# A buffer for each slot's row lists, the next slot's gathers ahead of the output writes, and a single tile's first product in two PSUM tiles

## The chip, the core and the metric

The kernel runs on one NeuronCore of a Trainium2 chip. Its engines work side by side, each through its own instructions in order: TensorE (PE in the profile; its weight loads are shown as PEld), VectorE (DVE), ScalarE (ACT), GpSimd (POOL) and SyncE (SP), which here issues most of the DMA transfers. GpSimd issues the indirect ones, which gather or scatter rows by a list of row numbers. Semaphores tie the engines together. The metric is the device time of one execution in microseconds (us).

## The reference

Attention with four sink tokens and a window of 128, over 4 batches, 8 heads, 768 positions and 64 dimensions, feeds a mixture of experts that gives each of the 3072 tokens to one of 8 experts:

```python
keep = is_sink | in_window                      # sink: pos < 4; window: 0 <= rel < 128
scores = np.where(keep, scale * q @ k.T, -1e9)
a = np.exp(scores - max); a = a / (a.sum(-1) + 1e-9)
x = (a @ v) -> (3072, 512)
...
logits = x @ w_gate                             # (3072, 8)
e_idx = argmax(logits); gate_w = softmax(logits)[e_idx]
eom = 1 / (1 + exp(-(x @ w_output_gate)))
for e in range(8):
    mask = e_idx == e
    h = np.maximum(x[mask] @ w1[e], 0)          # 512 -> 1024
    out[mask] = gate_w[mask, None] * eom[mask, e, None] * (h @ w2[e])   # 1024 -> 512
```

## The kernel before

**Stages.** The first half of the span is attention, a pair of heads at a time (`pair_step`), which leaves the token rows in a DRAM buffer `xd`, each with its output factor as a last column. Routing runs beside it. From about 180 us on experts are worked on, at first between the last attention steps, and from about 280 us on alone. Within the block around the whole stage (`manual_schedule`, L1285) each engine's instructions are issued in the order in which the program states them, so a line that stands earlier in the Python code stands earlier in its engine's queue.

**Work units.** `plan` (L720) lists the units of expert work. Entries 0 to 3 are early ones: 256 rows of each of the four experts that have most tokens. Entries 4 to 16 are thirteen slots of fixed size, which the device fills with experts at run time. `SIZES` (L37) counts a slot in units of 64 rows: 6 (three tiles of 128 rows), 4 (two tiles), 2 (one tile, a "single") and 1 (half a tile, a "half"). `SEQ` (L38) sets their order; by plan entry the tiles are 4: 3, 5: half, 6: 3, 7: single, 8: 2, 9: half, 10: 2, 11: single, 12: 2, 13: half, 14: 2, 15: single, 16: half. The last runs only where it is needed (L1434).

**Steps.** `steps` (L725 to L731) has for each entry a `first` (the product with w1 and the relu) and a `second` (the product with w2 and the writes). Products are made of three float32r products each, of high and low parts. `slots` (L1231) walks the steps. Between the pieces of a step it also places, at set times, the transposes of the next entry's rows (`to_x`, whose pieces are x_parts, L526, or half_x, L679). At the end of a step in which such transposes were placed it calls `rows_of` (L1193) for the entry after that one.

**Row lists.** `rows_of(k)` first lets SP load the row lists of entries up to k + 2 (`load_ids`, L736, L744 to L748: from the DRAM table `unitd` into the tile `idx`), those that are not there yet; then it issues the gathers of entry k (`gather`, L514): one indirect DMA of 128 rows per tile, on GpSimd, into one of three `xg` buffers (`XB`). Column 0 of a list serves the gather, column 1 or 2 the write. All slots' lists are parts of one tile, `idx` (L330).

**Writes.** `mm2_parts` (L662) yields behind each of 8 parts of the second product, and then, when it is asked once more, calls `put` (L652) for each tile: ScalarE scales the result into one of four `y` buffers, and GpSimd scatters it to `out` with an indirect DMA (L655). A three-tile entry makes its third tile's product and write first, the other two behind it.

**GpSimd's other work.** Weights come from DRAM by SP into four staging buffers (`raw`, L493). ScalarE casts the high part (L503), and VectorE, or GpSimd for one chunk in four, subtracts for the low part (L504). A split frees the staging buffer for the next load. The splits are placed between the steps' pieces by `supply` (L1041), by modelled times written into the program.

**The single tile.** `single_parts` (L611) makes the w1 product of one tile with the rows as the stationary side: two products of 512 columns, `products(0, ...)` and `products(1, ...)` (L616 to L622), each followed by a relu on VectorE (L602) and by a transpose (`turn`). Both write into one PSUM tile of two banks, which `s_tile` (L546) takes from a ring of two.

Of the kernel before, what the change touches and what calls it, by code (L numbers as in the profile page):

```python
# [10 lines left out]
I32 = mybir.dt.int32  # L11
# [7 lines left out]
P = 128  # L19
# [17 lines left out]
SIZES = (6, 6, 4, 4, 4, 4, 2, 2, 2, 1, 1, 1, 1)  # L37
SEQ = (0, 9, 1, 6, 2, 10, 3, 7, 4, 11, 5, 8, 12)  # L38
NSLOT = len(SIZES)
NT_MAX = 3  # L40
# [14 lines left out]
def moe_kernel(tc, qT, kx, vx, vs, wgo, w1, w2, nsink, window, out):  # L55
# [5 lines left out]
    nc = tc.nc  # L61
    ctx = ExitStack()
    with ctx:
        const = ctx.enter_context(tc.tile_pool(name="const", bufs=1))
        rt = ctx.enter_context(tc.tile_pool(name="rt", bufs=1))
# [261 lines left out]

        idx_e = rt.tile([P, 2, NE, 2], I32, name="idx_e")

        idx = rt.tile([P, NSLOT, NT_MAX, 4], I32, name="idx")  # L330
        lin_i = rt.tile([P, NSLOT], I32, name="lin_i")
        io8n = const.tile([P, E], F32, name="io8n")
        nc.vector.tensor_scalar(out=io8n, in0=io8, scalar1=float(NJP), scalar2=None, op0=ALU.mult)
# [180 lines left out]
        def gather(mp, ids, n=NTOK):  # L514
            xg = mp.tile([P, XW], F32, name="xg", bufs=XB)
            nc.gpsimd.indirect_dma_start(out=xg, out_offset=None, in_=xd[0:n + 1, :],  # L516
                                         in_offset=bass.IndirectOffsetOnAxis(ap=ids[0], axis=0))
            return xg, mp.tile([P, 1], F32, name="sc", bufs=6)
# [27 lines left out]
        def s_tile():  # L546
            return ps_s.tile([P, 2, 512], F32, name="s")

        def hidden(mp, xs):
            return [mp.tile([P, 2, xs[0].shape[-1]], F32R, name=name, bufs=4) for name in ("hh", "hl")]  # L550
# [49 lines left out]
        def relu(mp, ps):  # L600
            hr = mp.tile([P, 4, P], F32, name="hr", bufs=2)
            nc.vector.tensor_scalar(out=hr, in0=ps.rearrange("p (a b) -> p a b", b=P), scalar1=0.0, scalar2=None, op0=ALU.max)  # L602
            return hr

        def turned(hr):
            tp = ps_t.tile([P, 4, P], F32, name="tp")
            for f in range(4):
                nc.tensor.transpose(out=tp[:, f, :], in_=hr[:, f, :], identity=ident)
            return tp

        def single_parts(mp, w, xs, hs):  # L611

            (wh, wl), (xh, xl) = w, xs
            both = s_tile()

            def products(q, ds):  # L616
                qs = slice(q * 512, (q + 1) * 512)
                for d in ds:
                    wd, wld = wh[d][:, qs], wl[d][:, qs]
                    for i, (x, a) in enumerate(((xh, wd), (xh, wld), (xl, wd))):  # L620
                        nc.tensor.matmul(out=both[:, q, :], lhsT=x[:, d, 0:P], rhs=a,
                                         start=d == 0 and i == 0, stop=d == ND - 1 and i == 2)  # L622

            def turn(hr):
                tp = turned(hr)
                for a in range(2):
                    hi, lo = (x[:, :, 0:P] for x in hidden(mp, xs))
                    tpa = tp[:, 2 * a:2 * a + 2, :]
                    nc.scalar.copy(out=hi, in_=tpa)
                    tt(out=lo, in0=tpa, in1=hi.bitcast(F32), op=ALU.subtract)  # L630
                    hs.extend((hi[:, f, :], lo[:, f, :]) for f in range(2))

            products(0, range(2))
            yield
            products(0, range(2, ND))
            h0 = relu(mp, both[:, 0, :])
            yield
            products(1, range(3))
            yield
            turn(h0)  # L640
            products(1, range(3, ND))
            h1 = relu(mp, both[:, 1, :])
            yield
            turn(h1)

# [73 lines left out]

        plan = [(order_i[0:1, r:r + 1], [(idx_e[:, 0, r, j:j + 1], idx_e[:, 1, r, j:j + 1]) for j in range(2)], False) for r in range(NE)]  # L720
        for q in SEQ:
            cols = [[idx[:, q, i, j:j + 1] for j in range(3)] for i in range(-(-SIZES[q] // 2))]
            plan.append((exp_i[0:1, q:q + 1], cols, SIZES[q] == 1, q))
        n = len(plan) - 1
        steps = []  # L725
# [7 lines left out]
        queue = [k for f, k in steps if f == "first" and k > 2] + [n]  # L733
        there = set()

        def load_ids(q):  # L736

            at = nc.sync.value_load(lin_i[0:1, q:q + 1], min_val=0, max_val=(E - 1) * NJP + NJ)
            z = SIZES[q]
            for a in range(2):  # L740
                r = slice(a * U, (a + 1) * U)
                if z == 1:
                    src = unitd[:, bass.ds(at, 1), :]
                    nc.sync.dma_start(out=idx[r, q, 0:1, 0:2], in_=src[:, :, 0:2])  # L744
                    nc.sync.dma_start(out=idx[r, q, 0:1, 2:3], in_=src[:, :, 2 + a:3 + a])
                else:
                    src = unitd[:, bass.ds(at, z), :].rearrange("u (i a) c -> u i a c", a=2)
                    nc.sync.dma_start(out=idx[r, q, 0:z // 2, 0:2], in_=src[:, :, a, 0:2])  # L748


        mctx = ctx.enter_context(ExitStack())
# [10 lines left out]
        with ExitStack() as actx:  # L762
# [173 lines left out]
            def point(name=None):  # L936

                if later and name in (None, later[0][1]):
                    x = later[0]
                    x[1] = next(x[0], None)  # L940
                    if x[1] is None:
                        later.remove(x)
# [116 lines left out]
            def ensure(key):  # L1059
                while not all(x["key"] != key for x in items[n_put[0]:]) or key in todo:  # L1060
                    if n_put[0] == len(items):
                        while later:
                            point()
                        assert build()
                    place()
# [20 lines left out]
            def early_gather(k):  # L1086
                done = [after for after, m in ROUNDS for _ in range(m)][k] + 1
                return [gather(mx, [idx_e[:, 0, k, j:j + 1]], done * S) for j in range(2)]
# [104 lines left out]
            def rows_of(k):  # L1193
                ids = plan[k][1]
                while later and k >= NE:
                    point()
                for j in range(max(k, NE), min(k + AHEAD, len(plan))):
                    if j not in there and not later:
                        there.add(j)
                        load_ids(plan[j][3])  # L1200
                xgs[k] = early_gather(k) if k < NE else [gather(mx, a) for a in ids]
# [29 lines left out]
            def slots():  # L1231


                rest = None
                for i, (f, k) in enumerate(steps):
                    ensure((k, 0 if f == "first" else 1))
                    parts, costs = first(k) if f == "first" else second(k)
                    whole = sum(c for c, _ in costs)
                    tasks = []
                    if rest is not None:  # L1240
                        tasks.append((1.2, rest))
                        rest = None
                    j = queue[0]
                    follows = steps[i + 1:i + 3]
                    x = None
                    if plan[j][2]:
                        if j < len(plan) - 1 and f == "first" and follows[0] == ("first", j):
                            x = to_x(j)
                    elif f == "second" and ("first", j) in follows and not plan[k][2]:
                        x = to_x(j)  # L1250
                    if x is not None:
                        m = len(xgs[j])
                        end = whole - (0 if follows[0] != ("first", j) else 2.4)
                        tasks += [(max(0.1, end - 1.5 * (m - a)), x) for a in range(m)]
                    tasks.sort(key=lambda z: z[0])
                    t = 0.0
                    for n, (c, done) in enumerate(costs):
                        next(parts)
                        t += c
                        for _ in range(2):  # L1260
                            if tasks and tasks[0][0] <= t:
                                next(tasks.pop(0)[1], None)
                        yield c, done
                    for z in tasks:
                        next(z[1], None)
                    if f == "first" and len(xgs[k]) == 1:
                        rest = parts
                    else:
                        assert next(parts, None) is None
                    if x is not None:  # L1270
                        assert next(x, None) is None
                        queue.pop(0)
                        rows_of(queue[0])
                while n_put[0] < len(items) or todo:
                    if n_put[0] == len(items):
                        assert build()
                    place()
# [7 lines left out]
            with tc.manual_schedule(engines={ET.PE, ET.Activation, ET.DVE, ET.Pool, ET.SP}):  # L1285
                for i in range(NP + 2):
                    if i == NP:
                        qctx.close()
                        mp = mctx.enter_context(tc.tile_pool(name="mp", bufs=2, side="right", reuse_waits="tile"))
# [196 lines left out]
```

## Time and profile before

| | us |
|---|---|
| median of 3 runs | 582.18 (578.35 to 582.23) |
| the profiled execution | 580.31 |
| its span in the profile | 578.5 |
| TensorE busy | 513.3 (89%) |
| VectorE, ScalarE, GpSimd busy | 330.5, 269.5, 257.9 |
| TensorE's last product | 567.1 to 567.5 |

How to read the rows in the prediction. A row of the timeline has the start in us from the beginning of the span, the duration, the engine, the line of the kernel, the operation, output<-inputs and how often it follows in a row; in brackets the idle time of the engine just before it and what ended it. A row of the waits has the engine, the operation that waited, what it waited for, and then the sum in us, the number of waits and the longest. Releasers are inferred: where one instruction waits for several things, the row names the one that came last by the profile, which can be the wrong one. A row of the windows has the stretch in us and its length, then each engine's busy time with the number of instructions (PE, PEld, DVE, ACT, POOL), the granted TensorE clock as a share of full speed, the mean busy share of the 16 DMA engines, and what they moved in GB/s.

### The profile page before, as it was taken

How to read it: one execution, taken by the hardware profiler on the slowest of the kernel's cores; microseconds unless marked ns; L12 is line 12 of the kernel's file. 1: busy time of each engine (PE TensorE's matmuls, PEld its weight loads, DVE VectorE, ACT ScalarE, POOL GpSimd, SP SyncE). 2: the span in 40 equal slices, each digit the busy share in tenths (PEclk: the TensorE clock that was granted, in tenths of full speed). 3: DMA queues.
4: the chain of work that ended last, by engine and by line, in shares of the span. 5: the costliest groups of instructions: out<-in, count | busy, mean ns of one | idle time of the engine just before them, and what ended most of it. 6: DMA issues, size and time to landing. Idle time of an engine off the chain costs nothing. (4 is left out here: it accounts for less than half of the span.)

```text
span 578.5 us, 10477 instructions
## 1 busy us (share of the span) xinstructions
PE 513.3 (89%) x3432; PEld 390.0 (67%) x3432; DVE 330.5 (57%) x752; ACT 269.5 (47%) x721; POOL 257.9 (45%) x312
## 2 busy tenths in 40 slices
PE   3999999999979998998999999995999984799992
PEld 1566656666656753848899688984867964777971
DVE  5567698698867768994633424441644642544520
ACT  2576666666647220444534335541545442345420
POOL 4557756857856322635353313342512531513420
PEclk9999999999989998999999999998999996999997
DMA  6166775568987886337778665476586684866760
GB/s 228 61 134 187 145 151 169 142 139 213 192 247 121 205 210 205 106 113 256 229 226 312 240 195 156 139 264 246 183 291 214 226 267 178 265 224 224 253 227 19
DMA packets 72496, 112.83 MB, mean 195 GB/s; under 512 B 12044, under 2 KB 38672, under 8 KB 72434
## 3 DMA queue, kind: packets, MB, share of 16 engines
q1 hardware_dynamic: 67970, 98.16, 58.6%
q0 software_dynamic: 4464, 13.91, 6.6%
q8 instruction: 30, 0.49, 0.4%
q14 instruction: 32, 0.26, 0.2%
HBM read 98.28 MB, written 13.45 MB: 193 GB/s over the span
## 5 line engine op out<-in xcount | busy, mean ns | idle before, releaser
L833 ACT ACTIVATE e<-s,nmx 128x132 f32<-128x132 f32 x192 | 69.5, 366 | 67.2 <-DVE nmx L831 56.6
L821 PE MATMUL s<-kr,qr 64*128 64x260 f32 (+1 forms) x384 | 63.1, 430 | 16.2 <-ACT e L833 10.8
L821 PEld LDWEIGHTS s<-kr,qr 64*128 64x128 f32 x384 | 30.5, 198 | 40.2 <-ACT e L833 28.4
L544 DVE SCALAR_TENSOR_TENSOR hl<-s,hh 128x512 fp32r<-128x512 f32 (+1 forms) x32 | 24.2, 757 | 58.2 <-ACT hh L543 52.8
L655 POOL DMA_INDIRECT out_dram<-y,idx x20 | 24.4, 1219 | 59.1 <-DMA idx<-unitd 14.5
L543 ACT ACTIVATE hh<-s 128x512 fp32r<-128x512 f32 (+1 forms) x32 | 20.9, 652 | 61.7 <-PE s L563 56.5
L831 DVE TENSOR_REDUCE nmx<-s 128x2 f32<-128x264 f32 x96 | 41.5, 432 | 3.3
L537 DVE TENSOR_TENSOR xl<-tp,xh 128x512 fp32r<-128x512 f32 x21 | 14.4, 689 | 45.0 <-ACT xh L536 45.0
L808 POOL TENSOR_SCALAR qr<-qr 128x256 f32<-128x256 f32 x48 | 39.9, 850 | 0.4 <-DMA qr<-in_qT_dram 0.4
L85 POOL TENSOR_SCALAR_AFFINE_SELECT g<-f 128x512 f32<-128x512 f32 (+1 forms) x48 | 28.3, 589 | 21.7 <-DVE f L850 19.0
L833 ACT ACTIVATION_READ_ACCUMULATOR e<-s,nmx 128x1 f32 x192 | 37.6, 196 | 0.0
L827 DVE COPY_PREDICATED s<-maskf,s 128x256 f32<-128x256 int32 x80 | 33.7, 421 | 6.8 <-PE s L821 6.8
L844 PE MATMUL tp<-ident,e 128*128 128x128 f32 x192 | 30.2, 297 | 0.4 <-ACT f L848 0.4
L844 PEld LDWEIGHTS tp<-ident,e 128*128 128x128 f32 x192 | 22.1, 149 | 11.9 <-issue 4.7
L536 ACT CAST xh<-tp 128x512 fp32r<-128x512 f32 x21 | 12.3, 587 | 35.8 <-PE tp L534 35.8
L85 POOL TENSOR_SCALAR_AFFINE_SELECT f<-f 128x512 f32<-128x512 f32 (+1 forms) x48 | 27.0, 563 | 3.3
L655 POOL DMA_INDIRECT out_dram<-y,idx_e x8 | 10.0, 1254 | 39.0 <-ACT y L654 22.3
L534 PE MATMUL tp<-ident,xg 128*128 128x128 f32 x84 | 13.8, 291 | 14.9 <-DMA xg<-xd,idx 14.9
L516 POOL DMA_INDIRECT xg<-xd,idx x21 | 22.1, 1051 | 10.8 <-issue 5.5
L891 PE MATMUL oA<-f,vt 128*64 128x128 f32 x256 | 26.5, 285 | 0.4
L534 PEld LDWEIGHTS tp<-ident,xg 128*128 128x128 f32 x84 | 11.2, 151 | 19.0 <-issue 16.7
L848 ACT COPY f<-tp 128x512 f32<-128x512 f32 x32 | 18.6, 582 | 0.4 <-PE tp L844 0.4
(652 smaller groups left out, 1558.2 us busy)
## 6 DMA issues: line engine op xcount, KB each, us to landing
raw<-in_w_dram SPq DMA_DIRECT2D x88, 512.0 KB
kr<-in_kx_dram SPq DMA_DIRECT2D x16, 396.0 KB
qr<-in_qT_dram SPq DMA_DIRECT2D x16, 384.0 KB
vt<-in_vx_dram SPq DMA_DIRECT2D x16, 384.0 KB
xd<-x SPq DMA_DIRECT2D x16, 384.0 KB
a0h<-in_w_dram SPq DMA_DIRECT2D x4, 512.0 KB
a0l<-in_w_dram SPq DMA_DIRECT2D x4, 512.0 KB
b0h<-in_w_dram SPq DMA_DIRECT2D x3, 512.0 KB
```

Source lines behind the costliest of these rows:

```text
L85: nc.gpsimd.affine_select(out=ap, in_=ap if src is None else src, pattern=pattern, compare_op=op, fill=fill, base=base, channel_multiplier=cm)
L516: nc.gpsimd.indirect_dma_start(out=xg, out_offset=None, in_=xd[0:n + 1, :], in_offset=bass.IndirectOffsetOnAxis(ap=ids[0], axis=0))
L534: nc.tensor.transpose(out=tp[:, d, :], in_=xg[:, d * P:(d + 1) * P], identity=ident)
L544: nc.vector.scalar_tensor_tensor(out=lo, in0=ps, scalar=0.0, in1=hi.bitcast(F32), op0=ALU.max, op1=ALU.subtract)
L655: nc.gpsimd.indirect_dma_start(out=where, out_offset=bass.IndirectOffsetOnAxis(ap=ids, axis=0), in_=y, in_offset=None, bounds_check=rows - ...
L808: nc.gpsimd.tensor_scalar(out=q, in0=q, scalar1=SCALE, scalar2=None, op0=ALU.mult)
L821: nc.tensor.matmul(out=s[:, a, o0:P + CW], lhsT=z["q"][r, t * P:(t + 1) * P], rhs=z["k"][r, k0:k0 + P + CW - o0], start=True, stop=True)
L827: nc.vector.copy_predicated(out=both[:, :, 4:CW], mask=bc(maski[:, 1, 4:CW], 1, 2), data=s[:, :, 0:P])
L831: nc.vector.tensor_reduce(out=m, in_=both, axis=AX.X, op=ALU.max, negate=True)
L833: nc.scalar.activation(out=z["e"][:, t, a, :], in_=both[:, a, :], func=AF.Exp, bias=m[:, a:a + 1], scale=1.0, accum_out=z["rs"][:, t, a:a ...
L844: nc.tensor.transpose(out=tp[:, k, :], in_=z["e"][:, 2 * j + k // 2, k % 2, 4:CW], identity=ident)
L891: nc.tensor.matmul(out=o, lhsT=v[:, kt, r], rhs=src[:, kt, a, :], start=t == kt == 0 or t == kt + 1 == 4, stop=False, skip_group_check=True)
```

## The change

Three edits. First, `idx` becomes a list of tiles, one for each slot; the loads, gathers and writes index it accordingly. Second, at the end of a step in `slots`, the end of the transposes and `rows_of` for the next entry now stand ahead of the last piece of the step's own product, which for a `second` step holds the writes. Third, `single_parts` takes two tiles from the PSUM ring, and uses one bank of each, where it took one tile and used both its banks.

```diff
-        idx = rt.tile([P, NSLOT, NT_MAX, 4], I32, name="idx")
+        idx = [rt.tile([P, NT_MAX, 4], I32, name="idx%d" % q) for q in range(NSLOT)]
...
         def single_parts(mp, w, xs, hs):
 
             (wh, wl), (xh, xl) = w, xs
-            both = s_tile()
+            both = [s_tile()[:, 0, :] for _ in range(2)]
 
             def products(q, ds):
...
-                        nc.tensor.matmul(out=both[:, q, :], lhsT=x[:, d, 0:P], rhs=a,
+                        nc.tensor.matmul(out=both[q], lhsT=x[:, d, 0:P], rhs=a,
                                          start=d == 0 and i == 0, stop=d == ND - 1 and i == 2)
...
-            h0 = relu(mp, both[:, 0, :])
+            h0 = relu(mp, both[0])
...
-            h1 = relu(mp, both[:, 1, :])
+            h1 = relu(mp, both[1])
...
         for q in SEQ:
-            cols = [[idx[:, q, i, j:j + 1] for j in range(3)] for i in range(-(-SIZES[q] // 2))]
+            cols = [[idx[q][:, i, j:j + 1] for j in range(3)] for i in range(-(-SIZES[q] // 2))]
...
-                    nc.sync.dma_start(out=idx[r, q, 0:1, 0:2], in_=src[:, :, 0:2])
-                    nc.sync.dma_start(out=idx[r, q, 0:1, 2:3], in_=src[:, :, 2 + a:3 + a])
+                    nc.sync.dma_start(out=idx[q][r, 0:1, 0:2], in_=src[:, :, 0:2])
+                    nc.sync.dma_start(out=idx[q][r, 0:1, 2:3], in_=src[:, :, 2 + a:3 + a])
...
-                    nc.sync.dma_start(out=idx[r, q, 0:z // 2, 0:2], in_=src[:, :, a, 0:2])
+                    nc.sync.dma_start(out=idx[q][r, 0:z // 2, 0:2], in_=src[:, :, a, 0:2])
...
                     for z in tasks:
                         next(z[1], None)
+                    if x is not None:
+                        assert next(x, None) is None
+                        queue.pop(0)
+                        rows_of(queue[0])
                     if f == "first" and len(xgs[k]) == 1:
                         rest = parts
                     else:
                         assert next(parts, None) is None
-                    if x is not None:
-                        assert next(x, None) is None
-                        queue.pop(0)
-                        rows_of(queue[0])
```

## The prediction

> **What bounds the kernel now.** I read the page first, for the engine that fills the span.
>
> ```profile
> PE 513.3 (89%) x3432; PEld 390.0 (67%) x3432; DVE 330.5 (57%) x752; ACT 269.5 (47%) x721; POOL 257.9 (45%) x312
> ```
>
> TensorE is busy 89% of the span; no other engine passes 57%. So an edit counts by the TensorE idle time it removes, or makes, in the stretch it touches. All edited code belongs to the expert slots, which run from about 280 us on. So the second view is TensorE's waits in that stretch: total us, number, longest.
>
> ```profile
> PE tp L534 <- DMA xg<-xd,idx: 14.9, 2, 8.9
> PE tp L684 <- DMA xg<-xd,idx: 5.6, 3, 3.6
> PE s L621 <- DVE hr L602: 3.0, 3, 1.5
> ```
>
> Five waits for gathered token rows (xg) make 20.5 us; three inside the single-tile product make 3.0 us. Nothing in this list waits for weights. The third view is TensorE in order of time, cut to the rows with a large wait (start, duration, operation, idle before it and its releaser):
>
> ```profile
> 401.79 1.09 PE L534 MATMUL tp<-ident,xg 128*128 128x128 f32 x4 [5.99 <-DMA xg<-xd,idx]
> ...
> 471.61 0.50 PE L621 MATMUL s<-a0h,xh 128*128 128x512 f32 x1 [1.46 <-DVE hr L602]
> ...
> 484.71 1.08 PE L534 MATMUL tp<-ident,xg 128*128 128x128 f32 x4 [8.87 <-DMA xg<-xd,idx]
> ...
> 505.07 0.46 PE L684 MATMUL tp<-ident,xg 64*128 64x64 f32 x4 [3.57 <-DMA xg<-xd,idx]
> ```
>
> The rows wanted at 401.79 are plan entry 8's, at 484.71 entry 12's (each behind a single-tile slot, which is short), at 505.07 entry 13's. The fourth view is GpSimd in order of time, to see why these gathers were late.
>
> ```profile
> 384.62 2.39 POOL L504 TENSOR_TENSOR c4l<-raw,c4h 128x1024 fp32r<-128x1024 f32 x1 [5.31 <-ACT sc L531]
> 388.34 1.00 POOL L655 DMA_INDIRECT out_dram<-y,idx  x1 [1.33 <-ACT y L654]
> 393.54 0.98 POOL L655 DMA_INDIRECT out_dram<-y,idx  x1 [4.20 <-DMA idx<-unitd]
> 394.83 0.99 POOL L516 DMA_INDIRECT xg<-xd,idx  x1 [0.30 <-issue]
> ...
> 467.46 2.42 POOL L504 TENSOR_TENSOR b0l<-raw,b0h 128x1024 fp32r<-128x1024 f32 x1 [5.89 <-ACT b0h L503]
> 470.44 1.39 POOL L655 DMA_INDIRECT out_dram<-y,idx  x1 [0.56 <-ACT y L654]
> 476.69 0.98 POOL L655 DMA_INDIRECT out_dram<-y,idx  x1 [4.86 <-DMA out_dram<-y,idx]
> 477.98 0.99 POOL L516 DMA_INDIRECT xg<-xd,idx  x1 [0.30 <-issue]
> ```
>
> GpSimd works in program order. Two output writes stand ahead of each gather, and the second starts only 5.2 us (393.54 - 388.34) or 6.25 us (476.69 - 470.44) after the first: it waits for the first one's data to land, since both write `out`. The row at 393.54 names a load of row lists (idx) instead, but in the program that load comes behind the write, which cannot wait for it; I read it as the wait of the other row. The gather, ready long before, goes out 0.30 us behind the second write. That is the whole delay.
>
> **The moved gathers.** Ten of the `second` steps now ask for the next rows ahead of their last writes: 14 gathers, of entries 4, 5, 7, 8, 9, 11, 12, 13, 15 and 16. Only five waits exist to be removed; I take them in turn. From issue to landing a gather takes (min, median, max):
>
> ```profile
> DMA to landing us min/median/max: 3.9/5.8/7.5
> ```
>
> *Entry 8.* The gather follows c4l, which ends at 384.62 + 2.39 = 387.01, by 0.30: issued at 387.3 instead of 394.83. It lands between 391.2 and 394.8. TensorE wants it at 401.79 - 5.99 = 395.8, or, if the single-tile wait of the same slot goes too (one of the two under 1.46; about 0.8), at 395.0. Gain 6.0, nothing left.
>
> *Entry 12.* It follows b0l, which ends at 469.88: issued at 470.2 instead of 477.98. TensorE wants it at 475.84, or at 474.4 without the 1.46. It lands between 474.1 and 477.7, so between 0 and 3.3 us are left. What the DMA engines do in these stretches decides where between (columns behind the engines: granted clock, DMA share, GB/s):
>
> ```profile
> 386.00:388.00 2.00, 2.00 (x10) 1.64 (x10) 1.74 (x2) 1.47 (x2) 1.01 (x1) 1.00 0.21 80
> ...
> 396.00:398.00 2.00, 0.00 (x0) 0.00 (x0) 0.70 (x2) 0.00 (x0) 0.97 (x1) 1.00 0.97 348
> ...
> 470.00:472.00 2.00, 0.55 (x3) 0.34 (x3) 1.56 (x2) 0.74 (x2) 1.39 (x1) 1.00 0.35 136
> ...
> 480.00:482.00 2.00, 0.00 (x0) 0.00 (x0) 0.00 (x0) 0.00 (x0) 0.24 (x1) 0.50 1.01 381
> ```
>
> The late gathers met full DMA engines (0.97 and 1.01); the new places are ahead of those weight loads, at 0.21 and 0.35. I take a landing nearer to the shortest, about 5 us: 1.0 us is left, gain 7.9.
>
> *Entries 13, 9 and 5.* Each gather takes the place of a write in front of it:
>
> ```profile
> 310.88 1.03 POOL L655 DMA_INDIRECT out_dram<-y,idx_e  x1 [0.15 <-issue]
> ...
> 317.42 0.99 POOL L516 DMA_INDIRECT xg<-xd,idx  x1 [0.30 <-issue]
> ...
> 412.65 1.82 POOL L655 DMA_INDIRECT out_dram<-y,idx  x1 [0.15 <-issue]
> 414.78 0.97 POOL L516 DMA_INDIRECT xg<-xd,idx  x1 [0.30 <-DVE hl L544]
> ...
> 495.56 1.82 POOL L655 DMA_INDIRECT out_dram<-y,idx  x1 [0.17 <-issue]
> 497.69 1.83 POOL L516 DMA_INDIRECT xg<-xd,idx  x1 [0.30 <-issue]
> ```
>
> Entry 13 moves up 2.1 us against a wait of 3.57. If it lands as slowly as now 1.4 are left, at the median of 5.8 nothing; I take 0.7, gain 2.9. The other two waits at L684 are 5.6 - 3.57 = 2.0 together; entry 5 moves up 6.5 and entry 9 by 2.1, more than their waits. Gain 2.0.
>
> *The clock.* Behind the three long waits the granted clock is half:
>
> ```profile
> 401.70:406.50 4.80, 4.71 (x16) 3.94 (x17) 1.30 (x3) 1.72 (x5) 0.00 (x0) 0.50 0.00 1
> ...
> 484.60:489.20 4.60, 4.49 (x19) 3.84 (x19) 1.12 (x2) 1.52 (x5) 0.00 (x0) 0.57 0.00 0
> ...
> 505.00:510.00 5.00, 4.92 (x28) 4.74 (x28) 0.00 (x0) 0.56 (x2) 0.00 (x0) 0.66 1.04 395
> ```
>
> Busy time times the missing clock: 4.71 x 0.50 + 4.49 x 0.43 + 4.92 x 0.34 = 6.0 us. It appears behind waits of 3.57 us and more and not around the 1.46 (1.00 in the row from 470), so with at most about 1 us left it goes: 6.0. [...]
>
> *What the move costs.* The writes start about 1.3 us later per gather (0.99 + 0.30) where their y was ready. No one on the path reads `out`; what stands behind the writes on GpSimd is the weight splits (L504), and a split frees a staging buffer for which SP's next weight load waits. The tightest place:
>
> ```profile
> 449.75 0.99 POOL L516 DMA_INDIRECT xg<-xd,idx  x1 [0.30 <-issue]
> 453.04 1.00 POOL L655 DMA_INDIRECT out_dram<-y,idx  x1 [2.30 <-DMA out_dram<-y,idx]
> 454.06 2.43 POOL L504 TENSOR_TENSOR a2l<-raw,a2h 128x1024 fp32r<-128x1024 f32 x1
> ...
> SPq L493 <- POOL a2l L504: 4.8, 1, 4.8
> ...
> ACT c3h L503 <- DMA raw<-in_w_dram: 1.7, 1, 1.7
> ```
>
> Today the gather at 449.75, entry 11's, hides in a wait between two writes; ahead of both it pushes a2l, the load that waits 4.8 for it, and perhaps the cast that waits 1.7 for data, by up to 1.3 us. Entries 7's and 15's gathers lie between the same two kinds of write, so the bound is three times this, 3.9, and 0 from below: a write gains nothing from going later. I take 0.5, nearer to 0, because TensorE's list above has no wait for a cast or a split, even behind that 1.7. The other instructions of `rows_of` (register loads and row-list loads, all on SP) keep their place on SP, where the writes issue nothing.
>
> One thing speaks against entry 12's new place. Indirect DMAs take GpSimd 0.97 or 1.83 us in the rows above, and VectorE is busy with a split just there:
>
> ```profile
> 469.61 1.35 DVE L504 TENSOR_TENSOR b1l<-raw,b1h 128x1024 fp32r<-128x1024 f32 x1 [2.13 <-ACT b1h L503]
> ```
>
> The gather may be held to its end at 470.96, up to 0.8 us; the 0 to 3.3 left over covers it. [...]
>
> **A buffer per slot.** It adds no instruction. What it can remove is a wait of one slot's list load on another slot's reads, or the reverse.
>
> ```profile
> 389.30 1.49 SPq L748 DMA_DIRECT2D idx<-unitd  x2
> ```
>
> This load goes out at 389.3, though the write at 393.54, ahead of it in the program, has yet to read another slot's columns of the same buffer. So slots already pass one another, and every gather above shows only the 0.30 of its issue. Cost and gain 0. If the reversed order made the writes wait on the loads, separate buffers would prevent just that.
>
> **Two buffers in the single tile.** The second half's first product waits today until VectorE has read the first half, though it writes other columns: the row at 471.61. With two tiles that read is no longer in its way; VectorE's 0.7 us then lies beside nine products until the turn wants it. The second tile is the other buffer of a ring of two, whose last reader (a hidden-layer relu, or a write's scaling) finished a whole phase earlier. Gain 3.0.
>
> **Sum.** 6.0 + 7.9 + 2.9 + 2.0 + 6.0 + 3.0 - 0.5 = 27.3 us. What follows the last product (567.5 to 578.5) stays. The profiled execution took 580.31 us, 1.8 beyond its span and 1.9 below the median of the runs. It becomes 553.0; the median becomes 582.18 - 27.3 = 554.9. I forecast 555.
>
> **Rivals.** *Stalls shrink but stay.* If the earlier gathers meet weight loads and take 7.5, entry 12 keeps 3.3 and its slow clock (1.9), entry 13 keeps 1.4, and with TensorE running ahead the weight loads, which used the stalls at full DMA share, come due. Against the last: in 401.7 to 406.5 and 484.6 to 489.2 DMA stood at 0.00, all that was asked for having landed. If half of the 27 goes, 568.5.
>
> *It does not do what it says.* The moved gathers wait for something that shows only at the earlier time, such as row lists on SP behind weight loads, or a buffer. Lists are asked for two entries ahead, which speaks against it. Then the single-tile 3.0 remains: 579.
>
> *Slower: gathers block the writes.* A gather waits for one of three xg buffers, and now the writes, the splits and the weight loads stand behind it. One gather of today shows such a wait:
>
> ```profile
> 326.43 0.95 POOL L516 DMA_INDIRECT xg<-xd,idx  x1 [4.74 <-DMA raw<-in_w_dram]
> ...
> 325.21 0.46 PE L684 MATMUL tp<-ident,xg 64*128 64x64 f32 x4 [1.14 <-DMA xg<-xd,idx]
> ```
>
> (It names a weight load; the transposes that free its buffer ran just before, at 325.21.)
>
> Some 4.7 us at each of ten places and on to TensorE would cost 47, less 27: 602. It decides from 2.7 us a place on. Against it: the reading transposes are issued ahead of each moved gather, and only three-tile entries (4, among the moved) need all buffers.
>
> **From cases to numbers.** The sum as it stands 0.72, shrunken stalls 0.16, without effect 0.05, slower 0.07. The sum's own range: with nothing left over and no cost (27.3 + 1.0 + 0.7 + 0.5 = 29.5) and from the fastest run of before, 578.35, it is 548.9; with 3.3 left and its 1.9 of clock, 1.4 left and 3.9 cost, 19.0 remain (27.3 - 2.3 - 1.9 - 0.7 - 3.4): 563.2. To hold 8 in 10 the range goes into the shrunken case: 549 to 570. A change under 1%, 5.8 us, I call no change. Faster 0.88, same 0.05, slower 0.07.
>
> **What would show it.** Right: L534 and L684 wait under 3 us together for xg, the L621 waits are gone, each moved gather's row stands ahead of its writes, the clock shows no half-speed stretch after 390 us, except past the last product. Wrong: waits of TensorE for casts (L503) or splits (L504); a gather with some us of idle ahead of it and the writes behind; a DMA share near 1 with L534 still waiting.

## The result

The changed kernel takes 556.36 us (median of 4 runs, 555.80 to 556.95) against 580.26 us of the kernel before (4 runs, 576.67 to 582.23): 0.9595 of its time, 95% interval 0.9537 to 0.9653. Two later rounds of the same kernel gave 0.9562 [0.9507, 0.9617] and 0.9677 [0.963, 0.9725]. By the three pairs of medians it saves 23.9, 23.2 and 19.2 us. The ratios are taken from fast executions alone (a few fall into a slower state) and the medians from all, so a ratio is not quite the quotient of two medians. The profiled execution took 555.8 us, with a span of 554.1 (578.5 before).

Of the profile after, first the page's line of busy times:

```profile
PE 508.3 (92%) x3432; PEld 386.6 (70%) x3432; DVE 334.1 (60%) x752; ACT 269.3 (49%) x721; POOL 260.2 (47%) x312
```

TensorE does the same 3432 products in a span 24.4 us shorter; its busy time is 5.0 us less, mostly since fewer of them run at half clock (6.0 us of it before by the prediction's count, 1.7 now). TensorE's waits from 270 us on (total us, number, longest), whole up to a last one of 0.3:

```profile
PE tp L684 <- DMA xg<-xd,idx: 2.6, 2, 1.6
PE oA L710 <- ACT y L654: 1.6, 2, 0.8
PE tp L534 <- DMA xg<-xd,idx: 1.1, 1, 1.1
```

Of 20.5 us of waits for gathered rows 3.7 are left, and the three waits of L621 are gone. TensorE in order of time, the three rows that still wait for a gather (entries 9, 12 and 13):

```profile
409.87 0.46 PE L684 MATMUL tp<-ident,xg 64*128 64x64 f32 x4 [1.04 <-DMA xg<-xd,idx]
...
465.32 0.63 PE L534 MATMUL tp<-ident,xg 128*128 128x128 f32 x4 [1.08 <-DMA xg<-xd,idx]
...
481.81 0.46 PE L684 MATMUL tp<-ident,xg 64*128 64x64 f32 x4 [1.57 <-DMA xg<-xd,idx]
```

Entry 8 does not wait at all. GpSimd in order of time, at the two places that the prediction showed:

```profile
383.38 2.39 POOL L504 TENSOR_TENSOR c4l<-raw,c4h 128x1024 fp32r<-128x1024 f32 x1 [4.67 <-ACT sc L531]
385.93 0.99 POOL L516 DMA_INDIRECT xg<-xd,idx  x1 [0.16 <-issue]
387.23 0.97 POOL L516 DMA_INDIRECT xg<-xd,idx  x1 [0.30 <-issue]
388.50 1.02 POOL L655 DMA_INDIRECT out_dram<-y,idx  x1 [0.30 <-issue]
395.38 1.00 POOL L655 DMA_INDIRECT out_dram<-y,idx  x1 [5.86 <-ACT xh L536]
...
457.38 2.40 POOL L504 TENSOR_TENSOR b0l<-raw,b0h 128x1024 fp32r<-128x1024 f32 x1 [5.70 <-ACT b0h L503]
459.93 1.80 POOL L516 DMA_INDIRECT xg<-xd,idx  x1 [0.15 <-issue]
462.04 0.97 POOL L516 DMA_INDIRECT xg<-xd,idx  x1 [0.30 <-issue]
463.31 1.02 POOL L655 DMA_INDIRECT out_dram<-y,idx  x1 [0.30 <-ACT hh L629]
469.08 1.00 POOL L655 DMA_INDIRECT out_dram<-y,idx  x1 [4.74 <-PE oA L673]
```

The gathers stand directly behind the splits c4l and b0l, ahead of both writes. The writes are still 6.9 and 5.8 us apart (388.50 to 395.38, 463.31 to 469.08), each pair under other releasers' names than before. The profile has landing times for the first of each pair, 6.0 and 5.0 us behind its issue, and the second starts 0.8 us behind that: it waits for the first to land, as it did, but the gather that stood behind it in each pair is gone from there. One stretch of half clock is left, and the windows show it (stretch and its length, busy time and instructions of PE, PEld, DVE, ACT and POOL, granted clock, DMA share, GB/s):

```profile
480.00:482.00 2.00, 0.43 (x6) 0.23 (x5) 0.69 (x1) 0.79 (x2) 0.97 (x1) 1.00 0.96 326
...
484.00:486.00 2.00, 2.00 (x12) 2.00 (x11) 0.00 (x0) 0.00 (x0) 0.00 (x0) 0.50 1.01 345
```

It is behind entry 13's wait of 1.57 us, where the DMA share is 0.96 and 1.01.

To see where the time went, the same instructions of TensorE in both profiles (a transpose is a product with the identity, lines L534 and L608):

| TensorE reaches | before, us | after, us | difference |
|---|---|---|---|
| a transpose early in the expert stretch | 302.40 | 303.07 | +0.7 |
| a transpose ahead of entry 8's wait | 384.68 | 383.91 | -0.8 |
| the second transposes of entry 8 | 406.09 | 396.17 | -9.9 |
| a transpose between entry 9's and 12's waits | 435.94 | 425.81 | -10.1 |
| a transpose behind entry 12's wait | 488.82 | 467.75 | -21.1 |
| a transpose behind entry 13's wait | 515.11 | 491.85 | -23.3 |
| the end of the last product | 567.48 | 543.12 | -24.4 |

Nearly all of it comes at two places, entries 8 (9.1) and 12 (11.0), and some at entry 13 (2.2).

### The profile page after: what moved, and what is told of

Its sections match the earlier page's. It is cut to its first block, busy times and chain, and to the rows that moved or that the text cites. A ratio compares the mean times of both kernels' runs of the same rounds, so it can differ in the third digit from the quotient of the medians.

```text
span 554.1 us, 10479 instructions
## 1 busy us (share of the span) xinstructions
PE 508.3 (92%) x3432; PEld 386.6 (70%) x3432; DVE 334.1 (60%) x752; ACT 269.3 (49%) x721; POOL 260.2 (47%) x312
## 4 chain that ended last, share of the span: by engine, by line
PE 46%; DVE 17%; DMA 16%; ACT 8%; issue 7%; POOL 4%; SPq 1%; POOLq 0%; ACTq 0%; DVEq 0%
PE s L563 15%; PE oA L673 5%; DMA out_dram<-y,idx 5%; PE oB L673 5%; ACT e L833 4%; PE s L821 3%; DMA xg<-xd,idx 3%; DMA raw<-in_w_dram 3%; PE s L588 3%; DVE s L827 2%; DMA psk<-hl 2%; DVE nmx L831 2%; PE oA L710 2%; PE s L694 2%; PE oA L891 2%
## 5 line engine op out<-in xcount | busy, mean ns | idle before, releaser
L544 DVE SCALAR_TENSOR_TENSOR hl<-s,hh 128x512 fp32r<-128x512 f32 (+1 forms) x32 | 24.2, 756 | 54.3 <-ACT hh L543 52.1
L655 POOL DMA_INDIRECT out_dram<-y,idx x20 | 23.1, 1155 | 60.3 <-ACT hh L543 11.2
L516 POOL DMA_INDIRECT xg<-xd,idx x21 | 26.3, 1250 | 10.3 <-ACT xf L685 4.7
L655 POOL DMA_INDIRECT out_dram<-y,idx_e x8 | 9.1, 1136 | 34.9 <-ACT y L654 16.7
L654 ACT ACTIVATE y<-oA,sc 128x512 f32<-128x512 f32 (+1 forms) x16 | 10.4, 649 | 17.5 <-issue 4.6
L891 PEld LDWEIGHTS oA<-f,vt 128*64 128x64 f32 x256 | 14.4, 136 | 6.1 <-issue 3.3
```

What stands on the lines that cost most here:

```text
L655: nc.gpsimd.indirect_dma_start(out=where, out_offset=bass.IndirectOffsetOnAxis(ap=ids, axis=0), in_=y, in_offset=None, bounds_check=rows - ...
L891: nc.tensor.matmul(out=o, lhsT=v[:, kt, r], rhs=src[:, kt, a, :], start=t == kt == 0 or t == kt + 1 == 4, stop=False, skip_group_check=True)
```

## The experiments

Diffs are against the changed kernel, unless they say otherwise. Each ratio is to the kernel before, run on the same chip.

**The two PSUM tiles alone** (edit 3; lists and order as before). The diff is the `single_parts` part of the change.

> Only the third edit: the single tile's first product in two PSUM tiles; order and row lists as before. My theory: the three waits at L621 (3.0 us together) go and nothing else moves, so 3 us less than the kernel before (ratio 0.995); the five waits for gathered rows stay within 1 us of 14.9 (L534) and 5.6 (L684), since GpSimd's order is as before, and may take back part of it, because TensorE arrives earlier at rows that come no earlier. Rival, that the tiles matter through the ring of two buffers: new waits of TensorE at L563 or L694 behind a single tile, and no gain.

Measured 577.28 us, ratio 0.9948 [0.9921, 0.9974]. TensorE's waits of this run:

```profile
PE tp L534 <- DMA xg<-xd,idx: 17.5, 2, 10.1
PE tp L684 <- DMA xg<-xd,idx: 3.7, 3, 2.7
```

The L621 waits are gone, 3.0 us. The waits for rows grow from 20.5 to 21.2, and L534's 17.5 lies 2.6 above the 14.9, not within the 1 us expected; this fits a single tile that ends sooner and so meets its late gather sooner. By the times alone the edit is worth about 3 us. The profile doesn't show them, since the profiled execution was the slowest of ten, with a span of 578.6 us (578.5 before).

**The new order alone** (edit 2).

```diff
+                    if x is not None:
+                        ...
+                        rows_of(queue[0])
                     if f == "first" and len(xgs[k]) == 1:
                         rest = parts
                     else:
                         assert next(parts, None) is None
-                    if x is not None:
-                        ...
-                        rows_of(queue[0])
```

(against the kernel before)

> Only the second edit: gathers ahead of the writes, one tile for all row lists, one PSUM tile in the single. My theory: the separate lists do nothing, so this has the whole gain except the L621 waits: 20 to 22 us less than before (ratio 0.962 to 0.966), L621 waits about 3 us, GpSimd's writes as in the changed kernel. Rival, that the lists are needed by the new order: each write then waits for row-list loads that SP issues late, behind weight loads, several us at each of ten places, GpSimd's splits come later, and more than a third of the gain goes.

Measured 560.31 us, ratio 0.9658 [0.9605, 0.9711]. The waits:

```profile
PE s L621 <- DVE hr L602: 3.5, 3, 1.9
PE tp L684 <- DMA xg<-xd,idx: 2.6, 2, 1.7
```

The single tile's waits are as before, one of them now 1.91 us at 464.25 and followed by half clock from 464.72 to 468.13 (0.50 in the windows). No three-tile or two-tile entry (L534) waits for rows. So the order carries most of the gain.

**Order and tiles, without the lists** (edits 2 and 3, `idx` one tile as before).

> The changed kernel without the separate row lists (second and third edit). My theory: the same time as the changed kernel, 24 us less than before (ratio 0.957 to 0.962), with the same waits of TensorE: about 1 us for entry 12, 1.6 for entry 13, 1.0 for entry 9. Rival, that the lists carry part of the gain: 5 us or more above the changed kernel.

Measured 557.54 us, ratio 0.9600 [0.9535, 0.9665], that of the whole change. The waits for rows in its profile:

```profile
PE tp L684 <- DMA xg<-xd,idx: 1.8, 2, 1.0
PE tp L534 <- DMA xg<-xd,idx: 1.7, 1, 1.7
```

Entries 9, 12 and 13 wait 0.76, 1.71 and 1.00 us. GpSimd's idle time ahead of the second writes behind the gathers of entries 8 and 12 is 6.00 and 4.62 us with one tile, 5.86 and 4.74 with a list of them. A buffer for each slot does nothing here that these runs can tell.

**The gathers between the two writes.**

```diff
+        between = []
...
                 for s in part:
                     put(mp, ys[s], xgs[s][1], DM, out, NTOK, ids[s][1])
+                    if between:
+                        rows_of(between.pop())
...
-                        rows_of(queue[0])
+                        if f == "second":
+                            between.append(queue[0])
+                        else:
+                            rows_of(queue[0])
...
+                    if between:
+                        rows_of(between.pop())
```

> The changed kernel, but the moved gathers stand behind the first write of a pair and ahead of the second; behind a single tile's only write, as before. My theory, that the gathers were late only because of the second write's wait for the first one's landing (4 to 6 us): entry 8's gather goes out about 1.3 us behind the first write and its wait is gone or under 2 us; entry 12's keeps 2 to 4 us; entries 13 and 9 keep their 3.6 and 0.9. Sum 16 to 20 us less than before. Rival, that the gathers were late because the DMA engines are full with weight loads, whenever they are issued: the waits at L534 stay above 10 us together, and 3 to 8 us are gained.

Measured 565.98 us, ratio 0.975 [0.9704, 0.9795], 14.5 us below the kernel before by the ratio (0.025 x 580.82).

```profile
PE tp L534 <- DMA xg<-xd,idx: 5.6, 2, 4.3
PE tp L688 <- DMA xg<-xd,idx: 3.4, 2, 2.8
```

(L688 is L684 of the others.) Entry 12 waits 4.26 us, with half clock behind it from 474.83 to 478.24. What this gains, without a gather passing the first write, is the part that sat in the second write's wait for the first to land. It fell 1.5 us short of the 16 to 20 expected and is far above the 3 to 8 of the rival.

**Only entries 8 and 12 moved** (edits 1 and 3 kept).

```diff
-                    if x is not None:
+                    ahead = x is not None and queue[1] in (8, 12)
+                    if ahead:
...
+                    if x is not None and not ahead:
+                        assert next(x, None) is None
+                        queue.pop(0)
+                        rows_of(queue[0])
```

> The changed kernel with only entry 8's and entry 12's gathers (four of the fourteen) ahead of the writes; the others behind them as before. My theory: entries 13, 9 and 5 keep waits of about 3.6, 0.9 and 1.1 us and the half clock behind the first (1.7), and the rest of the gain is there: 20 to 22 us less than before, ratio 0.962 to 0.966. Rival, that the gain is spread over all moved gathers: 12 us or less.

Measured 562.62 us, ratio 0.965 [0.9594, 0.9705], beside the whole change's 0.9562 in the same round.

```profile
PE tp L684 <- DMA xg<-xd,idx: 5.5, 3, 2.8
PE tp L534 <- DMA xg<-xd,idx: 1.3, 1, 1.3
```

The half entries wait 5.5 us, as before the change (5.6), and half clock stands from 487.2 to 490.6, behind entry 13. The two large entries make the bulk, as the table above says.

**The changed kernel again**, timed in that round.

> The changed kernel itself, unchanged, on the same chip as the others of this call, for comparison: 0.9595 of before within 0.005.

Measured 560.10 us, ratio 0.9562 [0.9507, 0.9617]. Its profiled execution, with a span of 559.5, showed a wait that the first profile had not. GpSimd, VectorE, ScalarE and TensorE around it, in order of time:

```profile
433.48 1.39 POOL L655 DMA_INDIRECT out_dram<-y,idx  x1 [0.30 <-issue]
441.21 1.70 POOL L655 DMA_INDIRECT out_dram<-y,idx  x1 [6.33 <-ACT a3h L503]
447.53 0.98 POOL L655 DMA_INDIRECT out_dram<-y,idx  x1 [4.62 <-ACT hh L543]
448.52 2.42 POOL L504 TENSOR_TENSOR a2l<-raw,a2h 128x1024 fp32r<-128x1024 f32 x1
450.87 2.42 POOL L504 TENSOR_TENSOR c2l<-raw,c2h 128x1024 fp32r<-128x1024 f32 x1
...
448.24 6.15 DVE L504 TENSOR_TENSOR c1l<-raw,c1h 128x1024 fp32r<-128x1024 f32 x1 [0.25 <-ACT c1h L503]
...
454.88 1.05 ACT L503 CAST c3h<-raw 128x1024 fp32r<-128x1024 f32 x1 [5.73 <-DMA raw<-in_w_dram]
...
460.16 0.58 ACT L536 CAST xh<-tp 128x512 fp32r<-128x512 f32 x1
...
460.79 0.80 PE L621 MATMUL s<-a0h,xh 128*128 128x512 f32 x1 [2.77 <-ACT xh L536]
```

Three writes in a row, 7.7 and 6.3 us apart, bring GpSimd's split a2l to 448.52 (444.16 in the first profile), and c2l follows without a gap. VectorE's split c1l, which begins 0.3 us earlier than a2l, ends 1.1 us behind c2l: 6.15 us. In the first profile of the changed kernel the same split took:

```profile
448.20 1.21 DVE L504 TENSOR_TENSOR c1l<-raw,c1h 128x1024 fp32r<-128x1024 f32 x1
```

The late splits free their staging buffers late, so the next weights come late; ScalarE casts them in its order and only then casts the rows of entry 11, for which TensorE waits 2.77 us, with half clock from 459.98 to 466.8 behind it. It is this place, the split a2l, that the prediction called the tightest. The step from the late splits to the late weights is read from the order of the rows, not from an experiment of its own.

**The rows asked for in mid-step**, right behind the last transpose and not at the end of the step.

```diff
+                def ask(x):
+                    assert next(x, None) is None
+                    queue.pop(0)
+                    rows_of(queue[0])
...
                         for _ in range(2):
                             if tasks and tasks[0][0] <= t:
                                 next(tasks.pop(0)[1], None)
+                        if x is not None and not any(z[1] is x for z in tasks):
+                            x = ask(x)
                         yield c, done
                     for z in tasks:
                         next(z[1], None)
                     if x is not None:
-                        assert next(x, None) is None
-                        queue.pop(0)
-                        rows_of(queue[0])
+                        ask(x)
```

> The changed kernel, but a step asks for the next rows as soon as the current ones' last transpose is stated, in the middle of the step, so the gathers of entries 9, 12 and 13 stand ahead of the weight splits (a1l, b0l, a3l) too. My theory: the waits still left for rows (about 1.1 for entry 12, 1.6 for 13, 1.0 for 9, and 1.7 us of half clock behind the 1.6) are GpSimd's order again, so they go: 3 to 5 us less than the changed kernel, ratio to before 0.950 to 0.955. Rival, that the rest is the full DMA engines: the gathers go out several us earlier but land when they do now, under 1 us gained. Second rival: the splits, 1.3 us later per gather, or SP's row lists come in the way of weights, and TensorE waits at L563 or L673 for casts or splits.

Measured 555.02 us, ratio 0.9486 [0.9441, 0.9532], just below the range expected. All of TensorE's waits in its expert stretch:

```profile
PE oA L710 <- ACT y L654: 1.6, 2, 0.8
PE tp L608 <- DVE hr L602: 0.8, 2, 0.5
PE s L621 <- ACT xh L536: 0.6, 1, 0.6
PE s L621 <- DVE xl L537: 0.6, 1, 0.6
```

No wait for a gather is left, and no half clock between 268 us and the last product. As the intervals of this kernel and of the changed one overlap a little, both were timed once more side by side:

> The kernel that asks for the rows in mid-step, taken again beside the changed kernel, since the first comparison of the two (0.9486 against 0.9562, with intervals that overlap a little) leaves open whether it is faster. By the profiles it saves the changed kernel's three gather waits of the expert phase (1.04 + 1.08 + 1.57 us) and one stretch of half clock (1.7 us), less about 1 us of waits for casts of the rows: 3 to 5 us, ratio 0.948 to 0.952 where the changed kernel has 0.957. Rival: what it saves there is given back elsewhere, and the two agree within 0.2%.

> The changed kernel itself, on the same chip as the mid-step kernel: ratio 0.955 to 0.961, and 0.5 to 0.9 points above the mid-step kernel; by the rival the same as that.

Measured 551.34 us, ratio 0.9534 [0.9469, 0.9598], for the mid-step kernel and 559.66 us, ratio 0.9677 [0.963, 0.9725], for the changed one, both above their expected ranges. The profile of the mid-step kernel again has no wait for rows from 270 us on, that of the changed kernel 3.3 us of them. In both rounds the mid-step kernel is faster, by 0.8 and 1.4 points, 4.4 and 8.3 us; the second is more than the 3 to 5 expected. The two profiled executions of that round differ by 3.5 us of span (549.6 and 553.1); what makes the rest of the 8.3 isn't settled. The changed kernel's profile was taken of the fastest of its six executions (554.88, the others 558.55 to 561.22), so what the others lost is in no profile of that round. The mid-step kernel beats both the changed kernel and the one before.

**Twelve small operations on GpSimd behind the moved gathers**, ahead of the writes. They add work and take nothing away.

```diff
+        push = rt.tile([P, 64], F32, name="push")
+        nc.vector.memset(push, 0.0)
...
                         rows_of(queue[0])
+                        if f == "second":
+                            for _ in range(12):
+                                nc.gpsimd.tensor_scalar(out=push, in0=push, scalar1=SCALE, scalar2=None, op0=ALU.mult)
```

> The changed kernel with twelve small GpSimd operations on a scratch tile behind the moved gathers and ahead of the writes, at each of the ten places, some 3 to 4 us each, so that writes and splits come that much later: the cost that the slower rival supposes, tripled. My theory: nothing on the path waits for a write, and splits have room, so at most 3 us more than the changed kernel in all. Rival: the delay goes through to TensorE by splits and weight loads, 3 us or more at a place, 30 us in all, and TensorE waits for casts or splits.

Measured 574.45 us, ratio 0.9863 [0.9809, 0.9917], 14 us above the changed kernel of the same round (3.0 points by the ratios), where at most 3 us were expected. This expectation fell. The twelve took 5.4 to 8.3 us, not 3 to 4. GpSimd around entry 9's gather, and the two largest waits of TensorE (L658, L687 and L624 are L655, L684 and L621 of the others):

```profile
393.71 5.37 POOL L1275 TENSOR_SCALAR push<-push 128x64 f32<-128x64 f32 x12
399.54 1.05 POOL L658 DMA_INDIRECT out_dram<-y,idx  x1 [0.46 <-ACT xh L536]
407.23 0.99 POOL L658 DMA_INDIRECT out_dram<-y,idx  x1 [6.64 <-PE s L563]
408.23 2.42 POOL L504 TENSOR_TENSOR a1l<-raw,a1h 128x1024 fp32r<-128x1024 f32 x1
410.82 1.80 POOL L516 DMA_INDIRECT xg<-xd,idx  x1 [0.17 <-issue]
```

```profile
PE tp L687 <- DMA xg<-xd,idx: 8.7, 2, 4.5
PE s L624 <- ACT xh L536: 1.7, 1, 1.7
```

None of TensorE's waits names a write. But a short slot's step is not much longer than two writes that land one behind the other, so the gather of the entry after the next (9, 13) comes behind the second write and the split. Entries 9 and 13 wait 4.27 and 4.45 us, and half clock follows both, and once more the wait of 1.67 for entry 11's rows.

**The same twelve operations in the mid-step kernel**, to see whether the loss really comes back through those gathers.

> The twelve small GpSimd operations of the pushed variant, at the same place (ahead of a second product's last piece, and so ahead of its writes), but in the kernel that asks for the rows right behind the last transpose, in mid-step. Theory: what the pushes cost (14 to 17 us) came back through the gathers of the half entries 9 and 13, which stand on GpSimd behind the second of the delayed writes and behind a split (a1l, a3l). Asked for in mid-step they no longer stand behind that split (2.4 us and the idle time ahead of it), but still behind the second write, which is late by the pushes' 5.4. So the gather of entry 9 is issued near 405.6 instead of 399.8, lands near 411, and is wanted near 409: one wait of 1 to 3 us instead of 4.3, the same or somewhat more at entry 13, perhaps a stretch of half clock behind one of them. In all 3 to 10 us over the early kernel: ratio 0.954 to 0.966. Rival: the late splits hold up the weight loads and with them the casts and the products, wherever the gathers stand: the same 14 to 17 us over the early kernel, ratio 0.973 to 0.978, and waits of TensorE for casts or splits.

Measured 560.98 us, ratio 0.9648 [0.956, 0.9737]. That is 1.6 points above the mid-step kernel's first round, some 9 us, and 1.1 above its second, where the pushed kernel stood 3.0 above the changed one. By spans it is 6.2 us above the mid-step kernel's first profile (560.3 and 554.1), and the pushed kernel 10.8 above the changed one's of its own round (570.3 and 559.5). This kernel and the mid-step one did not run side by side, and the interval just reaches the 0.973 of the rival.

```profile
391.70 5.36 POOL L1281 TENSOR_SCALAR push<-push 128x64 f32<-128x64 f32 x12
397.52 1.05 POOL L658 DMA_INDIRECT out_dram<-y,idx  x1 [0.46 <-ACT xh L536]
404.39 1.08 POOL L658 DMA_INDIRECT out_dram<-y,idx  x1 [5.82 <-ACT y L657]
405.78 1.01 POOL L516 DMA_INDIRECT xg<-xd,idx  x1 [0.30 <-issue]
```

```profile
PE tp L687 <- DMA xg<-xd,idx: 2.9, 1, 2.9
PE s L624 <- ACT xh L536: 1.8, 1, 1.8
```

Entry 9's gather now comes ahead of a1l, 5.0 us sooner, and its wait, for which 1 to 3 us were expected, is gone; entry 13's is 2.86 instead of 4.45, with one stretch of half clock. The first write again starts 0.46 us behind the twelve operations, as in the pushed kernel, but the gather is sooner, and about half of the loss is gone. So where the next gather stands makes about half of what a late write costs; the intervals leave the share open, and the other half is not taken apart. The wait of 1.8 for entry 11's rows is that of the changed kernel's second profile (there 2.77), and stays.

## Why the prediction was right, and where it was off

The forecast was 555 us, 27.3 less than before. The medians are 556.36, 560.10 and 559.66 (the last two beside kernels before of 583.31 and 578.89), 19 to 24 us less, and by the ratios 19 to 26. The mechanism held; the sum was 2 to 8 us too large.

*What bounds it.* Right. The order alone gave 0.9658, the two tiles alone 0.9948, and their product, 0.961, is what both gave (0.9600). TensorE's waits for rows and at L621 fell by 19.8 us and its losses to half clock by 4.3, together 24.1 of the 24.4 us by which the profile's span fell.

*Why the gathers were late.* Right: with the gathers between the two writes, past the second write's wait but behind the first write, entry 12 waited 4.26 us, where it was 8.87 before and is 1.08 with both passed, so about 60% of the gain there lay in that wait. The second write starts 5.2 to 7.7 us behind the first in all pairs quoted. That a row naming the load of the lists is really the wait for the first write's landing, as the prediction read it, shows in another pair of the profile before, whose first write has a landing time: it is issued at 351.09 and lands 4.7 us later, and the second starts at 356.55, 0.8 behind, under the name of that load.

*Entry 8*, 6.0 with nothing left, and its clock: right, TensorE gained 9.1 us there, of which the terms were 6.0, 0.8 of the single tile and 4.71 x 0.50 = 2.4 of clock.

*Entry 12*, 7.9 with 1.0 left: right. 1.08 was left; the gather was issued at 459.93 and its rows were used at 465.19, 5.3 us later, where about 5 was taken. Its issue took 1.80 us instead of 0.97 and ended 0.87 us behind VectorE's split b1l, much as the prediction allowed, and the 1.08 lies within the 0 to 3.3 that it left open.

*Entries 13, 9 and 5*, 2.9 and 2.0: mis-sized by 1.9. Entry 13 kept 1.57 instead of 0.7, and entry 9 waited 1.04 instead of not at all; it had waited 0.86 before, so it gained nothing. Their gathers took 7.1 and 6.6 us to land (474.70 to 481.77, 403.26 to 409.83), near the longest of before (7.5), not its median. For entry 13 the prediction had the bound, 1.4, and took half of it; the row of its place, a DMA share of 1.04 just behind, spoke for the bound.

*The clock*, 6.0: mis-sized by 1.7. The step that failed is that half clock needs a wait like the 3.57 and is gone with 1 to 1.5 left. It stood behind the 1.57 of entry 13, and nothing was regained there: TensorE gained 2.2 us at this place, just the wait. That 3.3 us left at entry 12 would keep its 1.9 us of clock, a term of the range's slow end, no run shows; in the runs half clock stood behind waits from 1.57 us up, though not behind every longer one, and not behind entry 12's 1.08.

*The single tile*, 3.0: right. The waits of L621 for the relu are gone with the other edits and without them, and alone the edit gave 0.5%.

*What the move costs*, -0.5 (bounds 0 and 3.9): a cost that isn't constant. In the first and third profile of the changed kernel it did not show at all. In the second TensorE waited 2.77 us for the rows of entry 11 at the place that was named, and half clock over 6.8 us followed it, some 3 us more: beyond the bound. The bound counted only the 1.3 us by which a gather pushes a split; it missed that beside two splits on GpSimd close together one of VectorE took 6.15 us instead of 1.21, and it missed the clock. Whether the moved gather makes this likelier there isn't settled: in the profile before the split a2l came 13.3 us behind the first of the three writes, in the first after 11.4 and in the second 15.0, and the landing of the writes varies by more than the gather's 1.3.

*The first profile's own sum.* 27.3 less 0.9 and 1.0 for the waits left, less 1.7 for the clock and plus the 0.5 that did not show makes 24.2; measured 24.4.

*A buffer per slot*, 0: right; the whole change and the change without it agree (0.9595, 0.9600).

*Rivals.* That gathers block the writes did not come: each of the gathers quoted above starts 0.15 to 0.30 us behind what stands ahead of it. That the stalls shrink but stay came true in part: 3.6 us more of waits and clock were left in the first profile than the sum had, a quarter of the 13.6 that this rival took.

*The signs.* The waits for rows are 3.7 us together, not under 3; there is one half-speed stretch behind 390 us, not none; L621 no longer waits and the moved gathers stand ahead of their writes, as said. A DMA share near 1 with L534 still waiting, named as a sign of being wrong, was there too: the share was 1.07 from 464.24 to 465.32, during entry 12's wait of 1.08, and 0.99 and 0.96 during the two waits of L684. It cost little, since the waits were short.

## What to carry to other kernels

On a queue that runs in order, look at what a request stands behind, not only at when it is ready: a gather behind two writes to the same tensor paid here for the first write's landing (4.7 to 6.0 us behind its issue), and passing both was worth 3 to 4% here, asking in mid-step another 1%. Size what is left over of a removed stall by the landing times at the DMA share of the place to which the request comes (in the profile before, from 290 us on, the gathers with a landing time of 3.9 to 4.9 us had a mean share of 0.29 to 0.84 until they landed, those of 6.7 to 7.5 one of 0.89 to 1.05), and reckon with the chance of a stretch of half clock behind it (here 3.4 us at 0.50 behind TensorE waits from 1.57 us up, though not behind every longer one). When a write's delay looks free, follow it on its queue to the next request that stands behind it, in the step after this one.

## What the runs showed of the hardware

*Half clock behind short waits.* Stretches of 3.4 us at a granted clock of 0.50 stood behind single waits of TensorE of 1.57, 1.91, 2.77 (two in a row), 2.83, 2.86, 4.26, 4.27 and 4.45 us, and behind one of 1.67 with 0.56 more close by. None stood behind the waits of 0.76 to 1.48, nor behind ones of 1.71, 1.74 (twice), 1.76, 1.87, 2.74 and 2.79. So from 1.57 to 2.79 us it depends on something other than the wait's length. Within a profile the stretches start whole multiples of 3.41 us apart: before, at 399.85, 478.35 and 505.66, which are 23.0 and 8.0 times that. The wait of 1.57 lay inside one such interval (479.35 to 482.76), but so did that of 1.76 (457.09 to 460.50 in the mid-step kernel with the twelve operations), each counted back from its profile's half clock, and no half clock followed that one. What decides stays open.

*VectorE's splits beside GpSimd's work.* VectorE's split c1l, 1.21 us in the first profile of the changed kernel, took 6.15 in the second beside two of GpSimd's, though it is the one that begins first by the rows (by 0.28 us), and an indirect DMA's issue, 0.95 to 1.14 us elsewhere, took 1.80 at 459.93, where VectorE's split b1l was running:

```profile
458.70 2.16 DVE L504 TENSOR_TENSOR b1l<-raw,b1h 128x1024 fp32r<-128x1024 f32 x1 [1.07 <-ACT b1h L503]
```

It ends at 460.86, and the issue 0.87 us behind that. From 290 us on, in the profile before and the first one after, every issue longer than 1.2 us began while such a split of VectorE was running (9 and 12 of them), and ended 0.84 to 0.89 us behind that split. In the same two profiles every VectorE split longer than 1.3 us (11 and 9 of them) ran beside one or two of GpSimd's and ended 1.07 to 1.10 us behind the last of these, as the one of 6.15 did (1.10). Why is not taken apart.

*Two writes to one tensor.* The second write to `out` starts 5.2 to 7.7 us behind the first in the pairs quoted, and 0.8 us behind the first one's landing in the three for which a landing time is given above. What the wait costs is that landing, 4.7 to 6.0 us behind the first write's issue in these three.
